# Batch 0's queries and keys as whole float32 in the score products

## The chip, the core and the metric

The kernel runs on one core of a Trainium2 chip. The core has TensorE (matrix products, PE in the rows, its weight loads PEld), VectorE (DVE), ScalarE (ACT), GpSimd (POOL), SyncE (SP, which issues most DMAs) and 16 DMA engines. The metric is the device time of one execution in microseconds. It was run three times; the median counts.

## The reference

Attention with a sparse softmax over 4 batches, 8 heads, 576 positions and 64 dimensions, then two MLP layers on the 2304 tokens. What matters here is the first lines:

```python
scale = 1.0 / np.sqrt(q.shape[-1])
scores = scale * np.matmul(q, k.transpose(0, 1, 3, 2))
thresh = np.max(scores, axis=-1, keepdims=True) - tau
scores = np.where(scores >= thresh, scores, -1000000000.0)
scores = scores - np.max(scores, axis=-1, keepdims=True)
attn = np.exp(scores)
attn = attn / (np.sum(attn, axis=-1, keepdims=True) + 1e-09)
return np.matmul(attn, v).astype(np.float32)
```

Since scores are cut at a threshold of 0.02 below a row's maximum, they have to be nearly as exact as float32. Behind this stand `h = x @ w_in; g = h * clip(h + 3, 0, 6) / 6; g @ w_out` and a second layer with `g = h - tanh(h)`.

## The kernel before

**Units.** Attention goes by units of 128 queries of one head against all 576 keys. The 512 main queries of a head are four units; the last 64 queries of two heads j of a pair make one leftover unit (`h is None`). A batch has 36 units, in two halves g = 0 and 1 of the main queries: for each g and each pair of heads j, four units, and with g = 1 a leftover unit. There are 144 units.

**Queries and keys.** TensorE turns q and k so that the 64 dimensions lie on partitions (`k_round`, `q_round`, `q_left_round`; lines 561 and 577, PSUM tile tp). From tp they are split into two parts of type float32r, a high one (ScalarE, lines 584 and 591) and the rest (VectorE, lines 586 and 593). For k, both parts of a head lie on 128 partitions, 64 each. For q, GpSimd first copies the 64 columns beside themselves (line 554), so that after turning all 128 partitions hold the same queries twice; tile q holds the high part and the rest one behind the other. A product of 128 partitions with 288 columns then adds high q times high k and high q times the rest of k; a second one does the same with the rest of q. So a unit has four pieces on TensorE: two parts of q times two halves of 288 keys (line 678). A leftover unit has eight. Leftover queries go to tile qs, whose unused columns are zero.

**Softmax of a unit.** `softmax` writes the scores to one of two PSUM buffers s. VectorE reduces them to a negative maximum z (line 683), ScalarE makes the exponentials e with z as bias (line 685) and, for the first 54 units, the threshold (line 688); VectorE keeps the exponentials at or above the threshold (line 694), which is the last reader of s. ScalarE and GpSimd split e into two float16 parts pp (lines 699 and 705), a DMA turns them (pt<-pp, line 708), and `weighted` multiplies with v (line 731).

**What else runs.** `load_w` reads the 16 weight pieces of the first layer's first half; VectorE takes four operations of 512 columns for each (lines 418 to 426), while batch 0 is in work. From `layer1` on (lines 489 and 850), TensorE does the first half of the first layer for each half batch, between the units of later batches. The second half of the first layer and the second layer follow from about 490 us on.

**Order.** Every step is recorded as a task with an engine, a duration and a due time (`add`); `Plan.issue` runs a list scheduling with those numbers and emits the instructions in the order that comes out. The hardware runs each engine's instructions in that order; buffers in rings (`Ring`) make a task wait for the users of the buffer before.

Of the kernel before, what the change touches and what calls it, by code (L numbers as in the profile page):

```python
# [9 lines left out]
F32 = mybir.dt.float32  # L10
# [20 lines left out]
class Buf:  # L31


    def __init__(self, ring, prev):
        self.ring, self.prev, self.users, self.writers = ring, prev, [], []
        self.tile, self.slot, self.ends = None, None, []

    @property
    def t(self):
        if self.tile is None:  # L40
            self.tile = self.ring.make() if self.slot is None else self.ring.make(self.slot)
        return self.tile


# [156 lines left out]
def attention_moe_moe_kernel(  # L201
# [54 lines left out]
    add = plan.add  # L256

    LAG = 4
    STEP, SLOW, KNEE = 3.0, 0.8, 4
    LK, LQ, LV, LD = 5, 3, 1, 4  # L260
    XL, FO = 1, 7
# [259 lines left out]
    def load_q_left(b, half, key):  # L521

        t = QL[b, half] = R_ql.new()
        hs = slice(half * NP, (half + 1) * NP)
        for r in range(2):
            add("dma", 0.65, key, lambda r=r: nc.sync.dma_start(
                out=t.t[:, :, r, :], in_=q[b, hs, SM:S, :].rearrange("h p d -> p h d")), w=[t], xfer=0.37, slack=SB)

    def load_k(b, j, key):
        t = KR[b, j] = R_kr.new()  # L530
        add("dma", 0.6, key, lambda: nc.sync.dma_start(
            out=t.t, in_=k[b, 2 * j:2 * j + 2, 0:SM, :].rearrange("h (p c) d -> p h c d", c=NC)), w=[t], xfer=0.88, slack=SB)

# [11 lines left out]
    def load_q(b, g, j, key, eng="dma"):  # L545

        t = QR[b, g, j] = R_qr.new()
        queue = nc.sync if eng == "dma" else nc.scalar
        for i in range(2):
            add(eng, 0.47, key, lambda i=i: queue.dma_start(  # L550
                out=t.t[:, i, :, 0, :],
                in_=q[b, 2 * j + i, 0:SM, :].rearrange("(p c) d -> p c d", c=NC)[:, 2 * g:2 * g + 2, :]), w=[t], xfer=0.37, slack=SB)
        copy = lambda r: t.t[:, :, :, r, :].rearrange("p h c d -> p (h c) d")
        add("pool", 0.5, key + 4, lambda: nc.gpsimd.tensor_copy(copy(1), copy(0)), r=[t], w=[t])

    def transposes(ps, srcs):

# [6 lines left out]
    def k_round(b, j, part, key):  # L564

        if part == 0:
            KS[b, j] = R_k.new()
        ks, tp, kr, kl = KS[b, j], R_tp.new(), KR[b, j], KL[b]
        half = (slice(0, 64), slice(64, 128))
        n = (SM // 2, LF)[part]  # L570

        def tr():
            if part == 0:
                transposes(tp.t, [(kr.t[:, i, c:c + 2, :], 0) for i in range(2) for c in (0, 2)])
            else:
                for i in range(2):
                    nc.tensor.transpose(tp.t[0:64, i * LF:(i + 1) * LF], kl.t[:, 2 * j + i, :], ident[0:LF, 0:LF])

        add("pe", 2 * n * 0.00085, key, tr, r=[kr] if part == 0 else [kl], w=[tp, ks])
        for x in range(2 - part):  # L580
            cols = slice(x * n, (x + 1) * n) if part == 0 else slice(SM, S)
            out = lambda up, cols=cols: ks.t[half[up], :, cols]
            src = lambda x=x: tp.t[half[x], 0:2 * n].rearrange("p (i n) -> p i n", i=2)
            hi = add("act", t_act(2 * n), key + RK, lambda x=x, out=out, src=src: nc.scalar.activation(
                out=out(x), in_=src(), func=ACTF.Copy), r=[tp], w=[ks])
            add("dve", t_dve(2 * n), key + RK, lambda x=x, out=out, src=src: nc.vector.tensor_tensor(
                out=out(1 - x), in0=src(), in1=out(x).bitcast(F32), op=ALU.subtract), r=[tp], w=[ks], after=[hi])
# [8 lines left out]

    def q_round(b, g, j, key):

        qr, tp, qt = QR[b, g, j], R_tp.new(), R_q.new()
        add("pe", 4 * 0.11, key, lambda: transposes(  # L600
            tp.t, [(qr.t[:, i, c, :, :], 0) for i in range(2) for c in range(2)]), r=[qr], w=[tp, qt])
        q_split(qt, tp, lambda x: qt.t[:, x], 256, key)
        QT[b, g, j] = qt

    def q_left_round(b, j, key):

        ql, tp, qt = QL[b, 2 * j // NP], R_tp.new(), R_qs[j % 2].new()
        add("pe", 2 * 0.06, key, lambda: transposes(
            tp.t, [(ql.t[:, (2 * j + i) % NP, :, :], LF) for i in range(2)]), r=[ql], w=[tp, qt])
        q_split(qt, tp, lambda x: qt.t[:, x].rearrange("p (i n) -> p i n", n=LF)[:, 0:3:2, :], LF, key)  # L610
        QT[b, "l", j] = qt
# [50 lines left out]
    def softmax(u, key):  # L662
# [8 lines left out]
        s = lambda: ps.t[:, :, 0:SH]  # L671
        ex = lambda: e.t[:, n, :].rearrange("p (a s) -> p a s", a=2)

        def scores():
            ops = [(queries(b, g, j, x, c, part), KS[b, j].t[:, x % 2]) for x in hs for part in range(2)]
            for i, (l, ks) in enumerate(ops):
# [2 lines left out]
                        ps.t[:, half, 0:SH], l, ks[:, half * SH:(half + 1) * SH], start=i == 0, stop=i == len(ops) - 1,  # L679
                    )  # L680

        add("pe", 0.53 * len(hs), key, scores, r=[KS[b, j], QT[b, g if h is not None else "l", j]], w=[ps])
        add("dve", 0.69, key, lambda: nc.vector.tensor_reduce(  # L683
            out=z.t[:, 0:1], in_=s(), axis=AX.XY, op=ALU.max, negate=True), r=[ps], w=[z])
        exp = add("act", 0.66, key, lambda: nc.scalar.activation(  # L685
# [911 lines left out]
```

## Time and profile before

| | us |
|---|---|
| median of 3 runs | 1088.65 |
| runs | 1088.2 to 1093.36 |
| the profiled execution | 1088.51 |
| its span, first to last instruction | 1086.7 |
| TensorE busy in it | 1015.0 (93%) |
| VectorE busy | 847.6 (78%) |
| ScalarE busy | 718.6 (66%) |
| GpSimd busy | 339.0 (31%) |

Busy times are from the profiled execution and don't count waiting. The granted clock (PEclk) is the share of full speed that TensorE's clock had; its two levels are 1.2 and 2.4 GHz, so a mean between 0.5 and 1 is a mix. The mean of the whole execution is 0.964. In the 40 equal slices of the span, TensorE's granted clock stands at 0.6 to 0.8 in some of the first, and at 0.9 or more from the sixth on.

### The profile page before, as it was taken

What the parts mean: (1) busy time and instruction counts of PE and PEld (TensorE: products, weight loads), DVE (VectorE), ACT (ScalarE), POOL (GpSimd) and SP (SyncE); (2) the same over time, 40 slices, a digit from 0 to 9 for tenths busy, and PEclk for the clock granted to TensorE, in tenths of its full rate; (3) what the DMA queues carried; (4) which work ended last, traced back from release to release, by engine and by line L of the source; (5) the groups of instructions that cost most, each with busy time, mean ns of one, the idle gap of its engine ahead of it and who ended that gap; (6) DMA issues with size and microseconds to landing.
All of it is one profiled execution on the core that took longest, in us unless ns stands there. A gap on an engine that the chain in (4) does not pass through costs nothing.

```text
span 1086.7 us, 23294 instructions
## 1 busy us (share of the span) xinstructions
PE 1015.0 (93%) x8984; PEld 838.6 (77%) x8984; DVE 847.6 (78%) x1630; ACT 718.6 (66%) x1312; POOL 339.0 (31%) x353
## 2 busy tenths in 40 slices
PE   5668799999999899988999999999999999999998
PEld 4557788998999799978988888876676666666664
DVE  5889977687869788758797778889976796784564
ACT  6867979687967786645675566756755675574332
POOL 2656757666855675623000000000001111121000
PEclk8668899999999989998999999999999999999999
DMA  7899688967899989978657755432333866573335
GB/s 184 165 222 213 132 159 182 196 132 158 187 181 192 205 175 216 219 159 261 201 173 257 253 199 185 165 108 97 107 117 118 208 131 117 126 127 51 87 92 142
DMA packets 285007, 179.27 MB, mean 165 GB/s; under 512 B 202976, under 2 KB 257760, under 8 KB 284896
## 3 DMA queue, kind: packets, MB, share of 16 engines
q1 hardware_dynamic: 279088, 168.07, 61.0%
q0 software_dynamic: 5184, 9.44, 6.5%
q8 instruction: 71, 1.16, 0.5%
q14 instruction: 40, 0.33, 0.1%
q10 hardware_dynamic: 624, 0.26, 0.1%
HBM read 89.13 MB, written 46.14 MB: 124 GB/s over the span
## 4 chain that ended last, share of the span: by engine, by line
PE 58%; DVE 4%; ACT 1%; DMA 1%; issue 0%; SPq 0%; ACTq 0%; DVEq 0%
PE ya L489 24%; PE m L489 16%; PE h L489 10%; PE m L850 3%; PE s L678 2%; PE tp L731 1%; DMA y<-y 1%; PE h L850 1%; PE m L476 0%; DVE x L1276 0%; DMA st<-in_moe_w_in_dram 0%; DVE xh L1048 0%; DVE t L803 0%; PE tp L561 0%; DVE y L1175 0%
## 5 line engine op out<-in xcount | busy, mean ns | idle before, releaser
L705 POOL TENSOR_TENSOR pp<-e,pp 128x128 f16<-128x128 f32 (+3 forms) x156 | 181.1, 1182 | 120.3 <-issue 54.1
L489 PE MATMUL ya<-wo,g 128*128 128x512 f16 x864 | 205.4, 379 | 1.0 <-DVE g L813 0.6
L489 PEld LDWEIGHTS <-wi 128*128 128x128 f16 x1536 | 150.0, 98 | 40.4
L1416 POOL DMA_DIRECT2D po<-o x36 | 31.2, 876 | 459.7 <-ACT o L1410 459.7
L489 PEld LDWEIGHTS <-g 128*128 128x128 f16 x864 | 84.1, 98 | 79.3 <-DVE g L813 1.1
L683 DVE TENSOR_REDUCE z<-s 128x1 f32<-128x576 f32 x144 | 107.9, 753 | 45.4 <-PE s L678 44.7
L694 DVE SCALAR_TENSOR_TENSOR e<-s,z,e 128x576 f32<-128x576 f32 x144 | 115.8, 811 | 22.1 <-ACT e L685 17.1
L678 PE MATMUL s<-ks,q 128*128 128x288 f32 x512 | 105.9, 337 | 20.9 <-DVE e L694 20.1
L685 ACT ACTIVATE e<-s,z 128x576 f32<-128x576 f32 x144 | 105.0, 739 | 26.6 <-DVE z L683 20.3
L489 PE MATMUL m<-xT,ai 128*128 128x256 f32 (+1 forms) x720 | 112.8, 301 | 1.8 <-DVE st L426 0.6
L678 PEld LDWEIGHTS s<-ks,q 128*128 128x128 f32 x512 | 82.4, 212 | 29.4 <-DVE e L694 13.4
L489 PEld LDWEIGHTS m<-xT,ai 128*128 128x128 f32 x720 | 99.3, 190 | 3.7 <-DVE st L426 1.1
L489 PE MATMUL ya<-g,bo 128*128 128x256 f16 x864 | 101.1, 273 | 0.5 <-DVE g L813 0.5
L731 PE MATMUL tp<-vt,pt 128*128 128x65 f16 (+1 forms) x2240 | 88.4, 199 | 8.5 <-ACT q L591 2.4
L489 PE MATMUL m<-x,wi 128*128 128x256 f16 x768 | 95.2, 273 | 0.0
L731 PEld LDWEIGHTS <-pt 128*128 128x128 f16 (+1 forms) x2240 | 79.8, 104 | 16.7 <-DMA pt<-pp 6.0
L1381 ACT ACTIVATE t<-t,hid_s 128x512 f32<-128x512 f32 x72 | 51.6, 718 | 62.0 <-DVE t L1372 61.4
L489 PEld LDWEIGHTS <-bo 128*128 128x128 f16 x864 | 84.1, 98 | 10.6 <-issue 0.9
L489 PEld LDWEIGHTS <-bw 128*128 128x128 f16 x864 | 84.1, 98 | 10.4 <-issue 0.4
L813 DVE SCALAR_TENSOR_TENSOR g<-g,t 128x512 f16<-128x512 f16 x108 | 73.8, 686 | 20.7 <-ACT g L809 20.2
L809 ACT ACTIVATE g<-t 128x512 f16<-128x512 f32 x108 | 67.0, 624 | 33.7 <-DVE t L1383 26.0
L699 ACT ACTIVATE pp<-e 128x1152 f16<-128x1152 f32 (+1 forms) x80 | 85.1, 1064 | 5.0 <-DVE e L694 4.7
(177 smaller groups left out, 1878.0 us busy)
## 6 DMA issues: line engine op xcount, KB each, us to landing
st<-in_moe_w_in_dram SPq DMA_DIRECT2D x40, 512.0 KB, 5.0
st<-in_moe_w_out_dram SPq DMA_DIRECT2D x40, 512.0 KB, 4.4
xf<-xs SPq DMA_DIRECT2D x18, 512.0 KB, 5.2
y<-y SPq DMA_DIRECT2D x18, 512.0 KB, 3.8
po<-o POOLq DMA_DIRECT2D x36, 256.0 KB, 4.2
xs<-xT SPq DMA_DIRECT2D x8, 640.0 KB, 4.9
y<-ys SPq DMA_DIRECT2D x9, 512.0 KB, 5.9
po<-o SPq DMA_DIRECT2D x18, 256.0 KB, 2.0
```

Source lines behind the costliest of these rows:

```text
L489: nc.tensor.matmul(ps, l[a], r[b], start=first and t == 0 and i == 0, stop=last and t == 2 and i == n - 1,)
L678: nc.tensor.matmul(ps.t[:, half, 0:SH], l, ks[:, half * SH:(half + 1) * SH], start=i == 0, stop=i == len(ops) - 1,)
L683: add("dve", 0.69, key, lambda: nc.vector.tensor_reduce(out=z.t[:, 0:1], in_=s(), axis=AX.XY, op=ALU.max, negate=True), r=[ps], w=[z])
L685: exp = add("act", 0.66, key, lambda: nc.scalar.activation(out=ex(), in_=s(), func=ACTF.Exp, bias=z.t[:, 0:1]), r=[ps, z], w=[e])
L694: add("dve", 0.74, key, lambda: nc.vector.scalar_tensor_tensor(out=ex(), in0=s(), scalar=z.t[:, 1:2], in1=ex(), op0=ALU.is_ge, op1=ALU.mul ...
L699: high = add("act", t_act(w * S, sbuf=True), key, lambda: nc.scalar.activation(out=pp.t[:, 0:w, 0:S], in_=e.t[:, 0:w, :], func=ACTF.Copy), ...
L705: add(eng, dur, key, lambda src=src, dst=dst, queue=queue: queue.tensor_tensor(out=pp.t[:, 0:w, dst], in0=e.t[:, 0:w, src], in1=pp.t[:, 0: ...
L731: nc.tensor.matmul(pv.t[0:m, w_ * (D + 1):(w_ + 1) * (D + 1)], pt.t[:, n, blk, rows], vv, start=o == 0, stop=o == len(ops) - 1)
L809: hi = add("act", t_act(n, sbuf=True), key, lambda: nc.scalar.activation(out=gh(), in_=t(), func=ACTF.Copy, scale=GS2 if far else 1.0), r= ...
L813: go = lambda: nc.vector.scalar_tensor_tensor(out=gl(), in0=gh(), scalar=1.0 / GS2, in1=t(), op0=ALU.mult, op1=ALU.subtract)
L850: prev = [add("pe", t_mm(n, 1), kd, lambda p=p, l=l, r=r, m=m, s=s, ps=ps: nc.tensor.matmul(ps.t[:, 0:n], W["o", m].t[:, l, s], r[m].t[:, ...
L1381: add("act", t_act(2 * NB, sbuf=True, scalars=True), key, lambda: nc.scalar.activation(out=s_(), in_=h.t, func=ACTF.Tanh, scale=c), r=[h], ...
```

## The change

For batch 0 alone (`WHOLE = (0,)`), q and k are no longer split. Two heads of a pair are loaded beside each other (`pairs_of`, `cells`), so that one turn puts head 2j on partitions 0 to 63 and head 2j+1 on 64 to 127, and ScalarE alone takes the result out of tp into float32 tiles (names ksw and qw, in the same rings as before). A main unit is two products in float32 on the 64 partitions of its head, of 288 columns each. A leftover unit is two products on all 128 partitions; the leftover queries of the two heads stand in a block form in tile qw, whose other columns VectorE clears (`memset`). GpSimd's copy, VectorE's splits and the second load of leftover queries go. k's loads become two DMAs of one head each, in pieces of 64 values instead of 256.

```diff
     LAG = 4
+    WHOLE = (0,)
...
     def load_k(b, j, key):
         t = KR[b, j] = R_kr.new()
+        for i in range(2 if b in WHOLE else 0):
+            add("dma", 0.5, key, lambda i=i: nc.sync.dma_start(
+                out=cells(t)[:, :, i, :], in_=k[b, 2 * j + i, 0:SM, :].rearrange("(p c) d -> p c d", c=NC)), w=[t], xfer=0.44, slack=SB)
+        if b in WHOLE:
+            return
...
+    def pairs_of(t):
+        return t.t.rearrange("p i c r d -> p (i c r d)")[:, 0:4 * D].rearrange("p (c i d) -> p c i d", c=2, i=2)
+
+    def cells(t):
+        return t.t.rearrange("p i c d -> p (i c d)").rearrange("p (c i d) -> p c i d", c=NC, i=2)
+
+    def whole(ring, tag):
+        t = ring.new()
+        t.make = lambda: at_p.tile([128, 2, S] if tag == "ks" else [128, 2, 2, 256], F32, tag=tag, name=tag + "w", bufs=ring.n)
+        return t
...
     def k_round(b, j, part, key):
...
+        if b in WHOLE:
+            w = (SM, LF)[part]
+
+            def turn_whole():
+                if part:
+                    nc.tensor.transpose(tp.t[:, 0:LF], kl.t[:, 2 * j:2 * j + 2, :].rearrange("p i d -> p (i d)"), ident[0:LF, 0:LF])
+                for x, c in enumerate(() if part else ORDER):
+                    nc.tensor.transpose(tp.t[:, x * 128:(x + 1) * 128], cells(kr)[:, c].rearrange("p i d -> p (i d)"), ident)
+
+            add("pe", w * 0.00085, key, turn_whole, r=[kl if part else kr], w=[tp, ks])
+            add("act", t_act(w), key + RK, lambda: nc.scalar.activation(
+                out=ks.t[:, 0, part * SM:part * SM + w], in_=tp.t[:, 0:w], func=ACTF.Copy), r=[tp], w=[ks])
+            return
...
     def q_round(b, g, j, key):
 
+        if b in WHOLE:
+            qr, tp, qt = QR[b, g, j], R_tp.new(), whole(R_q, "q")
+            add("pe", 2 * 0.11, key, lambda: [nc.tensor.transpose(
+                tp.t[:, c * 128:(c + 1) * 128], pairs_of(qr)[:, c].rearrange("p i d -> p (i d)"), ident) for c in range(2)],
+                r=[qr], w=[tp, qt])
+            add("act", t_act(256, scalars=True), key + RK, lambda: nc.scalar.activation(
+                out=qt.t[:, 0, 0], in_=tp.t[:, 0:256], func=ACTF.Copy, scale=tau_b[:, 2:3]), r=[tp], w=[qt])
...
     def q_left_round(b, j, key):
 
+        if b in WHOLE:
+            ql, tp, qt = QL[b, 2 * j // NP], R_tp.new(), QT[b, 1, j]
+            clear = add("dve", 0.1, key, lambda: nc.vector.memset(qt.t[:, 0, 1, 0:2 * LF], 0.0), w=[qt])
...
+        def scores_whole():
+            rows = slice(0, 128) if h is None else slice(h % 2 * 64, h % 2 * 64 + 64)
+            qt, ks = QT[b, g, j].t, KS[b, j].t
+            l = qt[:, 0, 1, 0:2 * LF] if h is None else qt[rows, 0, 0, c % 2 * 128:c % 2 * 128 + 128]
+            for half in range(2):
+                nc.tensor.matmul(
+                    ps.t[:, half, 0:SH], l, ks[rows, 0, half * SH:(half + 1) * SH], start=True, stop=True)
+
...
-        add("pe", 0.53 * len(hs), key, scores, r=[KS[b, j], QT[b, g if h is not None else "l", j]], w=[ps])
+        add("pe", 0.98 if b in WHOLE else 0.53 * len(hs), key, scores_whole if b in WHOLE else scores, r=[KS[b, j], QT[b, g if h is not None else "l", j]], w=[ps])
```

The planner gets the new tasks with their durations and orders all of attention anew. Two places show it.

TensorE from the program's first product on, before the change (line 561 turns k and q, 577 the leftover keys, 628 is a sum for v, 678 the scores):

```order
L561 MATMUL tp<-ident,kr 128x128 x4
L561 MATMUL tp<-ident,qr 128x128 x4
L577 MATMUL tp<-ident,left 64x64 x4
L628 MATMUL tp<-vs,ones 128x1
L678 MATMUL s<-ks,q 128x288 x4
L561 MATMUL tp<-ident,kr 128x128 x4
L561 MATMUL tp<-ident,qr 128x128 x4
L678 MATMUL s<-ks,q 128x288 x4
L561 MATMUL tp<-ident,kr 128x128 x4
L577 MATMUL tp<-ident,left 64x64 x2
L678 MATMUL s<-ks,q 128x288 x8
```

The same place after the change (lines 606, 642 and 604 turn k, q and leftover keys, 690 is the sum for v, 741 the scores, whose two products are one main unit):

```order
L642 MATMUL tp<-ident,qr 128x128 x2
L606 MATMUL tp<-ident,kr 128x128 x4
L604 MATMUL tp<-ident,left 128x64 x2
L741 MATMUL s<-ksw,qw 128x288 x4
L690 MATMUL tp<-vs,ones 128x1
L606 MATMUL tp<-ident,kr 128x128 x4
L642 MATMUL tp<-ident,qr 128x128 x2
L604 MATMUL tp<-ident,left 128x64
L741 MATMUL s<-ksw,qw 128x288 x2
L606 MATMUL tp<-ident,kr 128x128 x4
L741 MATMUL s<-ksw,qw 128x288 x2
```

Four q turns become two, and the leftover keys of a pair one turn of 128 columns. The first scores stood behind four rows and are one unit; now they stand behind three and are two units.

VectorE from its first work on inputs on, before (586 and 593 are splits of k and q, 632 to 637 belong to v, 683 reduces and 694 masks):

```order
L586 TENSOR_TENSOR ks<-tp,ks 64x2x256 x2
L593 SCALAR_TENSOR_TENSOR q<-tp,tau_b,q 128x512
L586 TENSOR_TENSOR ks<-tp,ks 64x2x64 x2
L632 TENSOR_SCALAR vs<-tp 128x1
L634 TENSOR_SCALAR vs<-vs 128x1
L637 RECIPROCAL sv<-vs 128x2
L683 TENSOR_REDUCE z<-s 128x1 x2
L586 TENSOR_TENSOR ks<-tp,ks 64x2x256 x2
L593 SCALAR_TENSOR_TENSOR q<-tp,tau_b,q 128x512
L694 SCALAR_TENSOR_TENSOR e<-s,z,e 128x576
L586 TENSOR_TENSOR ks<-tp,ks 64x2x256
```

After (753 reduces, 764 masks, 694 to 699 belong to v):

```order
L753 TENSOR_REDUCE z<-s 128x1 x2
L694 TENSOR_SCALAR vs<-tp 128x1
L696 TENSOR_SCALAR vs<-vs 128x1
L699 RECIPROCAL sv<-vs 128x2
L764 SCALAR_TENSOR_TENSOR e<-s,z,e 128x576
L753 TENSOR_REDUCE z<-s 128x1
L764 SCALAR_TENSOR_TENSOR e<-s,z,e 128x576
L753 TENSOR_REDUCE z<-s 128x1
L764 SCALAR_TENSOR_TENSOR e<-s,z,e 128x576
```

All splits are gone, so that VectorE's first work on inputs is the reduction of the first two units.

VectorE over two units further on in batch 0, before (tiles m and st are the weight pieces, lines 418 to 426):

```order
L683 TENSOR_REDUCE z<-s 128x1 x2
L593 SCALAR_TENSOR_TENSOR q<-tp,tau_b,q 128x512
L694 SCALAR_TENSOR_TENSOR e<-s,z,e 128x576 x2
L418 TENSOR_SCALAR m<-m 128x512
L683 TENSOR_REDUCE z<-s 128x1
L420 TENSOR_SCALAR m<-m 128x512
L683 TENSOR_REDUCE z<-s 128x1
L423 SCALAR_TENSOR_TENSOR m<-st,m 128x512
L694 SCALAR_TENSOR_TENSOR e<-s,z,e 128x576
```

After, at the like place (419 to 427 are the weight pieces):

```order
L753 TENSOR_REDUCE z<-s 128x1 x2
L419 TENSOR_SCALAR m<-m 128x512
L764 SCALAR_TENSOR_TENSOR e<-s,z,e 128x576
L421 TENSOR_SCALAR m<-m 128x512
L764 SCALAR_TENSOR_TENSOR e<-s,z,e 128x576
L424 SCALAR_TENSOR_TENSOR m<-st,m 128x512
L753 TENSOR_REDUCE z<-s 128x1
L427 SCALAR_TENSOR_TENSOR st<-st,m 128x512
L753 TENSOR_REDUCE z<-s 128x1
```

The q split between two reductions and two masking steps is gone, and a step of the weights now stands between the two masking steps.

## Rows read from the trace of the kernel before

**Rows 1.** Stretches: busy us (instructions) of PE, PEld, DVE, ACT, POOL; clock, DMA share, GB/s.

```profile
10.00:80.00 70.00, 47.80 (x344) 40.02 (x342) 59.59 (x101) 54.87 (x105) 39.02 (x35) 0.66 0.89 194
80.00:120.00 40.00, 32.78 (x348) 28.90 (x349) 37.91 (x64) 32.65 (x71) 28.73 (x28) 0.87 0.89 196
...
140.00:200.00 60.00, 56.45 (x630) 53.12 (x629) 46.15 (x81) 49.93 (x105) 39.77 (x39) 1.00 0.81 175
200.00:480.00 280.00, 269.01 (x3042) 255.89 (x3037) 215.66 (x431) 207.23 (x388) 170.88 (x174) 0.99 0.88 182
```

**Rows 2.** Waits, 10 to 80 us: who waited for whom, us, times, longest.

```profile
PE s L678 <- DVE e L694: 10.9, 10, 2.6
...
DVE z L683 <- PE s L678: 5.0, 10, 1.9
```

**Rows 3.** Timeline: start us, us, instruction, [idle before and its releaser].

```profile
64.28 2.71 PE L678 MATMUL s<-ks,q 128*128 128x288 f32 x8 [1.12 <-DVE e L694]
...
67.03 0.76 DVE L683 TENSOR_REDUCE z<-s 128x1 f32<-128x576 f32 x1 [0.22 <-PE s L678]
...
69.16 1.54 DVE L694 SCALAR_TENSOR_TENSOR e<-s,z,e 128x576 f32<-128x576 f32 x2 [0.71 <-ACT z L688]
...
70.12 2.26 PE L678 MATMUL s<-ks,q 128*128 128x288 f32 x8 [1.56 <-DVE e L694]
...
75.84 2.26 PE L678 MATMUL s<-ks,qs 128*128 128x288 f32 x8 [2.61 <-DVE e L694]
```

**Rows 4.** Groups by line, 0 to 112 us; a line's durations; a timeline row.

```profile
L561 PE MATMUL tp<-ident,qr 128*128 128x128 f32 x32 | 7.6, 383 | 0.4 <-issue 0.3
...
L586 DVE TENSOR_TENSOR ks<-tp,ks 64x512 fp32r<-64x512 f32 x10 | 6.9, 689 | 4.0 <-ACT ks L584 3.8
L593 DVE SCALAR_TENSOR_TENSOR q<-tp,tau_b,q 128x512 fp32r<-128x512 f32 x8 | 6.0, 744 | 0.1
...
L586 DVE TENSOR_TENSOR ks<-tp,ks 64x128 fp32r<-64x128 f32 x4 | 1.1, 284 | 0.6 <-ACT ks L584 0.5
...
L593 DVE SCALAR_TENSOR_TENSOR qs<-tp,tau_b,qs x3: 340/342/343, 35.6 to 89.2; 128x128 fp32r<-128x128 f32 x3
...
4.24 0.30 DVE L880 MEMSET qs<- 128x128 f32 x2
```

**Rows 5.** Timeline of TensorE: a unit's scores and what follows, at either clock level.

```profile
47.78 1.30 PE L678 MATMUL s<-ks,q 128*128 128x288 f32 x4
48.88 1.76 PE L731 MATMUL tp<-vt,pt 128*128 128x65 f16 x28
...
119.04 0.69 PE L678 MATMUL s<-ks,q 128*128 128x288 f32 x4
119.57 0.28 PE L628 MATMUL tp<-vs,ones 128*128 128x1 f32 x2
```

**Rows 6.** Line 628, all of the span: records, ns min/median/max, first and last start.

```profile
L628 PE MATMUL tp<-vs,ones x32: 164/250/372, 10.1 to 391.5; 128*128 128x1 f32 x32
```

**Rows 7.** Timeline of the start.

```profile
8.91 0.75 DVE L593 SCALAR_TENSOR_TENSOR q<-tp,tau_b,q 128x512 fp32r<-128x512 f32 x1
...
10.51 1.31 PE L678 MATMUL s<-ks,q 128*128 128x288 f32 x4
...
11.86 0.76 DVE L683 TENSOR_REDUCE z<-s 128x1 f32<-128x576 f32 x1 [0.52 <-PE s L678]
...
14.53 0.76 DVE L683 TENSOR_REDUCE z<-s 128x1 f32<-128x576 f32 x1 [1.91 <-PE s L678]
```

**Rows 8.** DMA issues, 10 to 80 us: count, KB each, median us to landing.

```profile
kr<-in_k_dram SPq DMA_DIRECT2D x3, 256.0 KB, 4.2
```

**Rows 9.** Timeline of TensorE: scores on 128 partitions, then transposes from 64.

```profile
215.81 1.22 PE L678 MATMUL s<-ks,qs 128*128 128x288 f32 x8
216.95 0.33 PE L561 MATMUL tp<-ident,left 64*128 64x64 f32 x2
```

More of the change, by code (lines that the diff above doesn't have):

```diff
@@ L35, in __init__ @@
         self.ring, self.prev, self.users, self.writers = ring, prev, [], []
-        self.tile, self.slot, self.ends = None, None, []
+        self.tile, self.slot, self.ends, self.make = None, None, [], None
     @property
@@ L40, in t @@
         if self.tile is None:
-            self.tile = self.ring.make() if self.slot is None else self.ring.make(self.slot)
+            self.tile = self.make() if self.make else self.ring.make() if self.slot is None else self.ring.make(self.slot)
         return self.tile
@@ L524, in load_q_left @@
         hs = slice(half * NP, (half + 1) * NP)
+        if b in WHOLE:
+            add("dma", 0.65, key, lambda: nc.sync.dma_start(
+                out=t.t.rearrange("p h r d -> p (h r) d")[:, 0:NP, :], in_=q[b, hs, SM:S, :].rearrange("h p d -> p h d")),
+                w=[t], xfer=0.37, slack=SB)
+            return
         for r in range(2):
@@ L548, in load_q @@
         queue = nc.sync if eng == "dma" else nc.scalar
+        if b in WHOLE:
+            for i in range(2):
+                add(eng, 0.47, key, lambda i=i: queue.dma_start(
+                    out=pairs_of(t)[:, :, i, :],
+                    in_=q[b, 2 * j + i, 0:SM, :].rearrange("(p c) d -> p c d", c=NC)[:, 2 * g:2 * g + 2, :]), w=[t], xfer=0.37, slack=SB)
+            return
         for i in range(2):
@@ L566, in k_round @@
         if part == 0:
-            KS[b, j] = R_k.new()
+            KS[b, j] = whole(R_k, "ks") if b in WHOLE else R_k.new()
         ks, tp, kr, kl = KS[b, j], R_tp.new(), KR[b, j], KL[b]
@@ L570, in k_round @@
         n = (SM // 2, LF)[part]
+        if b in WHOLE:
[8 more added lines that the diff above has]
+                out=ks.t[:, 0, part * SM:part * SM + w], in_=tp.t[:, 0:w], func=ACTF.Copy), r=[tp], w=[ks])
+            return
         def tr():
@@ L597, in q_round @@
     def q_round(b, g, j, key):
+        if b in WHOLE:
+            qr, tp, qt = QR[b, g, j], R_tp.new(), whole(R_q, "q")
[4 more added lines that the diff above has]
+                out=qt.t[:, 0, 0], in_=tp.t[:, 0:256], func=ACTF.Copy, scale=tau_b[:, 2:3]), r=[tp], w=[qt])
+            QT[b, g, j] = qt
+            return
         qr, tp, qt = QR[b, g, j], R_tp.new(), R_q.new()
@@ L605, in q_left_round @@
     def q_left_round(b, j, key):
+        if b in WHOLE:
+            ql, tp, qt = QL[b, 2 * j // NP], R_tp.new(), QT[b, 1, j]
+            clear = add("dve", 0.1, key, lambda: nc.vector.memset(qt.t[:, 0, 1, 0:2 * LF], 0.0), w=[qt])
+            add("pe", 0.06, key, lambda: nc.tensor.transpose(
+                tp.t[:, 0:LF], ql.t.rearrange("p h r d -> p (h r d)")[:, 2 * j % NP * D:(2 * j % NP + 2) * D], ident[LF:2 * LF, LF:2 * LF]),
+                r=[ql], w=[tp, qt])
+            for i in range(2):
+                half = slice(i * 64, i * 64 + 64)
+                add("act", t_act(LF, scalars=True), key + RK, lambda i=i, half=half: nc.scalar.activation(
+                    out=qt.t[half, 0, 1, i * LF:(i + 1) * LF], in_=tp.t[half, 0:LF], func=ACTF.Copy, scale=tau_b[half, 2:3]), r=[tp], w=[qt], after=[clear])
+            QT[b, "l", j] = qt
+            return
         ql, tp, qt = QL[b, 2 * j // NP], R_tp.new(), R_qs[j % 2].new()
```

## The prediction

> **What bounds the kernel now.** I read the stretches of the profile first, since one busy share over 1087 us mixes stages with different limits. From 200 to 480 us TensorE works 269 of 280 us at clock 0.99, and from 140 to 200 us 56.45 of 60 at 1.00: there the end is set by how much TensorE still has to do. From 10 to 80 us, nearly all of batch 0's attention, it works only 47.80 of 70 us, and at a granted clock of 0.66, a mix of the 1.2 and the 2.4 GHz level. VectorE has 59.59 of 70 us there and 37.91 of 40 from 80 to 120 us [rows 1]. So the change, which lies wholly in batch 0, takes work from the engine that is full and gives work to the one that has room.
>
> Next the waits. From 10 to 80 us the scores waited 10.9 us in ten places for VectorE's masking step (e, line 694), which frees their PSUM buffer; VectorE's reductions waited 5.0 us for scores [rows 2]. The two form a loop, and the timeline shows a lap: eight score pieces (two units) start at 64.28, VectorE reduces the second unit at 67.03, ScalarE's exponential and threshold come between, masking starts at 69.16 and the next eight pieces at 70.12; the lap after starts at 75.84. That is 5.84 and 5.72 us for two units, 2.9 us a unit [rows 3]. A lap holds VectorE's work and the scores' own time. Shortening the first and lengthening the second is exactly what the change does, so the two have to be weighed against each other.
>
> **What is removed from VectorE.** In batch 0 go eight k splits of 512 columns at 0.689 us, four of 128 columns at 0.284, eight q splits at 0.744 and four for leftover queries at 0.342 [rows 4]: 5.5 + 1.1 + 6.0 + 1.4 = 14.0 us. Added are four clears of 128 columns; two like them took 0.30 us [rows 4], so 0.6 us. Net 13.4 us. By VectorE's order two of the large and two of the small k splits and one q split stand ahead of the first reduction: 2 x 0.689 + 0.744 + 2 x 0.284 = 2.7 us. Six large and two small k splits, five q and two leftover splits follow before the 20th masking step, which the trace has at about 77 us: with two clears, 4.1 + 0.6 + 3.7 + 0.7 - 0.3 = 8.8 us. Two q splits, two leftover splits and two clears remain after it: 1.9 us.
>
> **What TensorE gets.** A unit of 128 queries has four pieces of 288 columns today and needs two products in whole float32. Today's pace: four pieces at 47.78 are followed by the next work at 48.88, 1.10 us at 1.2 GHz; at 119.04 and 119.57, 0.53 us at 2.4 GHz [rows 5]. No row shows a wide float32 product. The narrow one of line 628 is 16 instructions in the program and 32 records in the trace [rows 6], so one product is two records and a unit stays at four. From below, a record costs no more than today's piece: then nothing is added. From above it costs twice that. I take the upper end: today each piece fills 128 partitions with the halves of one operand, so two stationary loads cover the four partial products of 64 rows each; the new product has 64 partitions of plain values, and the same four partial products need twice the streamed columns. A unit is then 1.06 us at the high level and 2.20 at the low. The four leftover units are unchanged: eight pieces for two heads become two products over all 128 partitions, 8 x 0.13 = 1.06 either way. So 32 x 0.53 = 17.0 us is added if all runs at 2.4 GHz and 32 x 1.10 = 35.2 us if at 1.2. Sixteen q transposes of 128 columns go, 0.24 us each as this stretch ran them [rows 4], 3.8 us; the leftover ones go from 24 to 12 and are left out.
>
> The Trainium skill (FP8 and Floating Point Precision, section TensorE Precision Notes) says true FP32 is four passes through the array. By it two products of 288 columns would be 2304 columns, 0.96 us at 2.4 GHz, an estimate; that would make the addition 13.8 instead of 17.0 us.
>
> **Which clock.** With 20 units' scores added, TensorE's 47.80 us of 70 become about 62 to 66. The trace shows a stretch with 32.78 of 40 us busy at clock 0.87 and those above 90% at 0.99 to 1.00 [rows 1], so I expect 10 to 80 us at about 0.87. A score unit is then 1.06 / 0.87 = 1.2 us. Today at 0.66 it lies between 0.53 and 1.10, about 0.9. It grows by 0.3 us, not by 1.1.
>
> **The sum.** *Start:* the first scores stand at 10.51, behind a q split that ends at 9.66 and k splits, and the reductions at 11.86 and, after a wait of 1.91, at 14.53 [rows 7]. With the splits gone the scores come some 2 us earlier; they then take about 1 us longer for the first unit, and k comes by two DMAs whose second issue costs some half microsecond. Of 2.7 us I enter 1.0. *10 to 80 us:* 8.8 us less on VectorE. With two score buffers, 0.3 us more per unit lengthens the lap of two units by 0.3, so 0.15 a unit and 3.0 us for 20. Net 5.8. *80 to 120 us:* 1.9 us less on VectorE, but here the first MLP layer already shares TensorE: 32.78 us plus 16 x 0.53 = 8.5, less about 4 from the clock going from 0.87 to 1.0, is 37 of 38 us. It fills up; I enter 0. Together 6.8 us. Behind that TensorE is full and its instructions for batches 1 to 3 and the layers are the same, so the shift is carried to the end: 1088.5 us of the profiled execution (span 1086.7 and 1.8 around it) become 1081.7. The median of the runs is 1088.65, 0.1 us from it.
>
> **Entered at nothing.** ScalarE loses half of its eight wide k copies and half the columns of the q copies and gets four small ones; it has 54.87 of 70 us [rows 1] and gains at most what VectorE doesn't need. GpSimd loses eight q copies of its 39.02 of 70. The k loads come in 256-byte pieces instead of 1 KB: 256 KB took 4.2 us to land [rows 8], issued well ahead of their use; only the first pair is waited for. Below nothing is excluded, since the bytes are the same; if the DMA engines, at 0.89 from 10 to 80 us [rows 1], are filled by the extra pieces, up to 2 us are lost. The planner orders all of attention anew, since it holds other durations; rows like those of the kernel before can move by a wait or two of 1 to 3 us in either direction, which the range holds.
>
> A switch of the array also has to be priced. Between eight score pieces at 215.81 and transposes of 64 partitions at 216.95 [rows 9], 8 x 0.132 = 1.06 us of streaming ends at 216.87: the switch costs at most 0.08 us, and 64 switches 5 us of TensorE time, inside the room above. The Trainium skill (TensorEngine Tiling (Array Packing), section Key Properties) has a rule against this change: changing the tiling mode drains TensorE. By the row that drain would take 5 us out of the forecast's room and at worst out of the gain; the trace neither shows a longer one nor scores on 64 partitions.
>
> **Rivals.**
> *The whole relief comes through* (0.15). Float32 records are no longer than today's pieces, so laps shrink by all of VectorE's work: 1.0 + 8.8 + 1.9 = 11.7 us, 1076.8 us. For it: two records, as the trace has. Against it: the four partial products above.
> *The scores take it all back* (0.25). The change does what it says, but the clock stays at 0.66: a unit's scores go from 0.9 to about 1.8 us, 0.45 per unit in the lap, 9 us over 20 units against 8.8. With the start's 1.0 left, about 1088 us. For it: TensorE still waits in every lap, which is when the low level was granted. Against it: it waits less than before.
> *TensorE becomes the bound* (0.17), the slower one. At 1.2 GHz, 10 to 80 us needs 47.80 + 20 x 1.10 - 3 = 66.8 us, and the 10.9 us of waiting for the masking step [rows 2] can't be filled in program order: 77.7 instead of 70, 7.7 us later. In 80 to 120 us another 5 of the 6.5 us added don't fit, since its idle time lies in waits too. Less 1.0 at the start, 1088.5 + 11.7 = 1100 us. It decides once TensorE is over 95% busy in 10 to 80 us with the clock below about 0.7.
> *The forecast* (0.43): 1081.7 us, its own range 1078 to 1086.
>
> **The numbers.** A difference under 0.5%, 5.4 us, can't be told from none by this measurement: 1083.2 and 1094.1 are the limits. Of the forecast's 0.43 some 0.32 lie below 1083.2; with 0.15 of the first rival and a trace of the second that makes 0.48 faster. The rest of the forecast and most of the second give 0.33 for no change. The third and a little of the second give 0.19 slower. The range runs from 1075 to 1097: it cuts a little of the first rival and about half of the third.
>
> **What would show it.** VectorE about 13 us less in all, nearly all before 120 us. Two records per float32 score product, a unit's four at about 1.06 us at the high level. Granted clock of 10 to 80 us above 0.8. The first reduction before 11.5 us, and 20 masking steps done near 71 us instead of 77. TensorE's total changed by less than the 17 us, since the rest of batch 0 runs at the higher clock. The forecast is wrong if TensorE isn't full from about 130 us on, if laps stay at 2.9 us a unit, or if a wait of several microseconds appears behind batch 0 that isn't there now.

## The result, and the profile after

The changed kernel takes 1103.3 us (median of 6 runs, 1102.4 to 1105.21), the kernel before on the same chip 1089.33 (1088.2 to 1093.36): 1.0126 times as long, 95% interval 1.0107 to 1.0144, or 14 us more. The forecast was 1081.7, its range 1075 to 1097. The third rival, "TensorE becomes the bound", had said 1100.

The stretches of the profile after, columns as in [rows 1]:

```profile
10.00:80.00 70.00, 58.74 (x275) 36.85 (x275) 45.08 (x78) 46.98 (x92) 32.93 (x26) 1.00 0.77 166
80.00:120.00 40.00, 35.98 (x266) 26.27 (x265) 32.49 (x53) 26.72 (x59) 23.02 (x22) 1.00 0.74 166
...
140.00:200.00 60.00, 56.76 (x637) 53.37 (x637) 44.32 (x80) 52.16 (x110) 43.23 (x42) 0.98 0.75 161
```

From 10 to 80 us VectorE fell from 59.59 to 45.08 us busy and TensorE rose from 47.80 to 58.74; neither is full, and fewer VectorE instructions fit into the stretch (78 instead of 101). The waits of the same 70 us, against [rows 2]:

```profile
DVE z L753 <- PE s L741: 25.6, 15, 5.6
...
PE s L741 <- DVE e L764: 9.1, 8, 2.3
```

VectorE's reductions now wait 25.6 us for scores, where they waited 5.0; the scores wait about as long for the masking as before. A lap of one unit shows why (timeline of TensorE and VectorE, against [rows 3]):

```profile
15.06 2.28 PE L741 MATMUL s<-ksw,qw 64*128 64x288 f32 x4
17.27 1.11 PE L606 MATMUL tp<-ident,kr 128*128 128x128 f32 x4
...
18.92 2.29 PE L741 MATMUL s<-ksw,qw 64*128 64x288 f32 x4 [0.53 <-DVE e L764]
...
21.24 0.76 DVE L753 TENSOR_REDUCE z<-s 128x1 f32<-128x576 f32 x1 [2.38 <-PE s L741]
21.91 0.81 DVE L764 SCALAR_TENSOR_TENSOR e<-s,z,e 128x576 f32<-128x576 f32 x1
...
22.78 2.29 PE L741 MATMUL s<-ksw,qw 64*128 64x288 f32 x4 [0.53 <-DVE e L764]
```

Scores start at 18.92, are reduced at 21.24, the unit before them is masked at 21.91 (it stands behind the reduction in VectorE's order), and the next scores start at 22.78: 3.86 us a unit, 2.2 of them scores. Before it was 2.9.

One number in these rows misleads. The clock reads 1.00 from 10 to 120 us, but the durations are those of 1.2 GHz: four transposes take 1.11 us at 17.27, and a score unit 2.2 us. In the kernel before, four transposes take 1.09 us where its clock reads 0.50:

```profile
22.81 1.09 PE L561 MATMUL tp<-ident,qr 128*128 128x128 f32 x4 [0.32 <-issue]
```

Here is TensorE later in the profile of the changed kernel:

```profile
116.10 1.20 PE L741 MATMUL s<-ksw,qw 64*128 64x288 f32 x4
117.23 1.02 PE L801 MATMUL tp<-vt,pt 128*128 128x65 f16 x28
...
119.60 0.60 PE L589 MATMUL tp<-ident,kr 128*128 128x128 f32 x4
```

The same four records take 1.13 us to the next start, and four transposes 0.60. By durations the high level was first granted near 110 us, and before the first record of a change the view shows 1.00. In the kernel before this touches only the time up to some 15 us: its 0.66 from 10 to 80 us would be about 0.62 (an estimate, with those 5 us counted as 0.50).

The start, against [rows 7], and the records of line 741, against [rows 6]:

```profile
9.99 0.76 DVE L753 TENSOR_REDUCE z<-s 128x1 f32<-128x576 f32 x1 [5.60 <-PE s L741]
...
11.91 0.76 DVE L753 TENSOR_REDUCE z<-s 128x1 f32<-128x576 f32 x1 [1.16 <-PE s L741]
```

```profile
L741 PE MATMUL s<-ksw,qw x144: 402/684/847, 7.7 to 144.8; 64*128 64x288 f32 x128, 128*128 128x288 f32 x16
```

The first two reductions come 1.9 and 2.6 us earlier; 72 products are 144 records, as said. Landmarks, with the masking steps counted in VectorE's rows:

| | first reduction | 20th masking ends | 36th (batch 0's last) | 144th | span |
|---|---|---|---|---|---|
| before | 11.86 | 77.6 | 137.1 | 475.0 | 1086.7 |
| after | 9.99 | 86.3 | 149.3 | 488.5 | 1100.6 |

Batch 0 lost 14 us from its start to its end; behind it the loss stayed between 11 and 15.

### The profile page after: what moved, and what is told of

Same layout as the page of the kernel before. It is cut to its first block, busy times and chain, and to the rows that moved or that the text cites. A ratio compares the mean times of both kernels' runs of the same rounds, so it can differ in the third digit from the quotient of the medians.

```text
span 1100.6 us, 23154 instructions
## 1 busy us (share of the span) xinstructions
PE 1047.0 (95%) x8944; PEld 845.1 (77%) x8944; DVE 837.7 (76%) x1610; ACT 714.3 (65%) x1312; POOL 333.9 (30%) x345
## 4 chain that ended last, share of the span: by engine, by line
PE 53%; DVE 2%; ACT 1%; issue 0%; ACTq 0%; DVEq 0%
PE ya L490 25%; PE m L490 14%; PE h L490 10%; PE m L920 2%; PE h L920 1%; PE m L477 1%; PE tp L801 1%; PE s L748 0%; DVE t L1442 0%; DVE x L1346 0%; ACT x L1344 0%; PE m L470 0%; DVE t L1453 0%; ACT t L1451 0%; DVE g L883 0%
## 5 line engine op out<-in xcount | busy, mean ns | idle before, releaser
L490 PE MATMUL m<-xT,ai 128*128 128x256 f32 (+1 forms) x720 | 115.3, 306 | 1.3 <-DVE t L873 0.8
L490 PEld LDWEIGHTS m<-xT,ai 128*128 128x128 f32 x720 | 101.6, 195 | 4.5 <-DVE t L873 2.3
L801 PE MATMUL tp<-vt,pt 128*128 128x65 f16 (+1 forms) x2240 | 90.7, 202 | 3.9 <-DVE q L634 2.2
L741 PE MATMUL s<-ksw,qw 64*128 64x288 f32 (+1 forms) x144 | 68.8, 628 | 14.5 <-DVE e L764 13.4
L748 PE MATMUL s<-ks,q 128*128 128x288 f32 x384 | 72.3, 313 | 8.1 <-DVE e L764 7.6
```

What stands on the lines that cost most here:

```text
L490: nc.tensor.matmul(ps, l[a], r[b], start=first and t == 0 and i == 0, stop=last and t == 2 and i == n - 1,)
L741: nc.tensor.matmul(ps.t[:, half, 0:SH], l, ks[rows, 0, half * SH:(half + 1) * SH], start=True, stop=True)
L748: nc.tensor.matmul(ps.t[:, half, 0:SH], l, ks[:, half * SH:(half + 1) * SH], start=i == 0, stop=i == len(ops) - 1,)
L801: nc.tensor.matmul(pv.t[0:m, w_ * (D + 1):(w_ + 1) * (D + 1)], pt.t[:, n, blk, rows], vv, start=o == 0, stop=o == len(ops) - 1)
```

## Experiments: what kept the clock low

The theory after this profile: products on 64 of the array's 128 partitions left TensorE at the low level. First the changed kernel with one line other, every engine's order kept; each unit gets the sum of two heads' scores:

```diff
-            rows = slice(0, 128) if h is None else slice(h % 2 * 64, h % 2 * 64 + 64)
+            rows = slice(0, 128)
```

> The changed kernel in the same order on every engine; only its float32 score products of batch 0 take all 128 partitions instead of 64, so that each unit gets the sum of the scores of two heads (this part of the output is not the reference's). Theory, half-filled array: products on 64 partitions leave TensorE at the low level, and at 128 partitions it gets the high one as in the kernel before; a score unit falls from 2.2 to about 1.1 us in most of 20 to 110 us and the time to about 1080 to 1086 us, as I had forecast. Rival, doubled columns and the order: rows don't matter, the unit stays at 2.2 us until 110 us and the time within 2 us of 1103.

Measured: 1088.23 us (10 runs, 1084.41 to 1092.11), 0.997 of before (0.9949 to 0.999). Its stretches:

```profile
10.00:80.00 70.00, 48.63 (x354) 33.52 (x353) 57.09 (x96) 54.65 (x111) 41.52 (x33) 0.85 0.90 197
80.00:120.00 40.00, 34.51 (x324) 28.41 (x322) 37.86 (x64) 34.06 (x75) 27.17 (x29) 0.92 0.90 210
```

The clock rises from 11 us on, and the 36th masking ends at 131.8 instead of 149.3. That is the whole loss and 5.3 us more, from partitions alone. TensorE is even less busy from 10 to 80 us than in the changed kernel (48.63 against 58.74 us), so its idle time is not what had kept the clock low. The time is 2 us above the range I gave: not all of the 5.3 arrive at the end.

Then the products by themselves, with no other engine between them (`s` alternates between two pairs of PSUM banks; `half` are the two halves of the partitions):

```python
for u in range(U):        # stretch 1: halves in turn; 2: all 128; 3: half[0] alone
    for x in range(2):
        nc.tensor.matmul(s[u % 2][:, x, 0:SH], weights[0][half[u % 2], :], kw[half[u % 2], ends[x]], start=True, stop=True)
```

> A kernel of its own that computes nothing of the reference: five stretches of score-like products on TensorE alone, back to back, each after some 20 us of rest: 24 units of two float32 products of 288 columns on 64 partitions (halves of the array in turn), the same on 128 partitions, on 64 partitions of one half; then 48 units of two float32r products on 64 partitions in turn and on 128. Theory, half-filled array: the first, third and fourth stay at 1.2 GHz to their end (2.2 us a float32 unit, 0.55 a float32r one), the second and fifth start so and go to half of it (1.1 and 0.28) within a few microseconds. Rival, only the gaps between the products kept the clock low: all five speed up when nothing interrupts them.

Busy us (records) of TensorE and its clock in each stretch, cut where the clock changes:

```profile
16.80:21.30 4.50, 4.50 (x19) 1.00 0.00 0
21.30:31.00 9.70, 9.70 (x80) 1.00 0.01 2
44.80:48.60 3.80, 3.77 (x8) 0.50 0.01 2
48.60:70.20 21.60, 21.60 (x89) 1.00 0.00 0
83.30:129.80 46.50, 46.44 (x96) 0.50 0.00 0
```

The third stretch shows it most plainly: 46.44 us without a gap on one half of the array, and the clock stays at 0.50 to the end, 0.48 us a record, 1.93 a unit. On 128 partitions it rises early, and a record then takes 0.243 us, a unit 0.97. The first stretch missed my expectation: two halves in turn run at the same time, 19 records in 4.5 us at the low level and 80 in 9.70 at the high, 0.12 each, and the clock rises. (The 1.00 of its first 4.5 us is again the view before a first record.) The fourth, float32r in turn, missed it in the same way; the second and the fifth came as expected. The Trainium skill (TensorEngine Tiling (Array Packing), section Key Properties) says that tiles operate independently; the first stretch agrees (0.12 us a record in turn, 0.243 on 128 partitions).

Does more work around them help? The changed kernel with two products on all partitions behind each unit:

```diff
+            for half in range(2):
+                nc.tensor.matmul(ps.t[:, half, SH:512], qt[:, 0, 0, 0:128], ks[:, 0, 0:512 - SH], start=True, stop=True)
```

> The changed kernel in its own order; behind each whole score unit of batch 0 stand two float32 products of 224 columns on 128 partitions, whose result nobody reads. That is 0.78 of a unit's columns on top, 1.7 us a unit at 1.2 GHz and 0.85 at 2.4. Theory, the clock follows how much of the array works: with these the high level is granted from early on, a unit with its filler takes about 1.9 us, less than the 2.2 of the changed kernel without it, and the time is 1092 to 1103. Rival, products on 64 partitions run at that pace whatever stands around them: a unit takes 3.9 us, and with 36 units the time is above 1140.

Measured: 1127.48 us (2 runs), between the two expectations. At 64.17 a unit takes 2.22 us to the filler and the filler 1.65; the high level first comes near 57 us instead of 110, and does not stay. Inconclusive: the rise came earlier, but not early enough to pay.

## Experiments: what a score unit's length is worth

The changed kernel in its own order with q and k rounded to float32r, each product twice (four pieces a unit) and once (two); both leave out the low halves:

```diff
-[128, 2, S] if tag == "ks" else [128, 2, 2, 256], F32, tag=tag
+[128, 2, S] if tag == "ks" else [128, 2, 2, 256], F32R, tag=tag
-            for half in range(2):
+            for n, half in ((0, 0), (0, 1), (1, 0), (1, 1)):     # once: ((1, 0), (1, 1))
```

> The changed kernel in the same order, but q and k of batch 0 are rounded to one float32r value each and every score product is made twice on 64 partitions, so that a unit has four pieces of 288 columns as before the change (the low halves of q and k are left out). Theory, doubled time of scores: a unit takes 0.53 to 1.1 us, VectorE keeps its relief, and the time is 1077 to 1084. Rival, the loads in 256-byte pieces and the new order: these stay, and the time stays above 1095. If 64 partitions keep the clock low, units show 1.1 us up to 100 us, not 0.53.

> The changed kernel in its own order with q and k of batch 0 rounded to one float32r value, each product made once: a unit has two pieces of 288 columns on 64 partitions (the low halves are left out). Theory, a lap of two units holds one unit's scores: at the low level a unit takes 0.55 us, where four pieces take 1.1 and the whole float32 ones 2.2; half of 0.55 us x 36 units, 10 us, moves the 36th masking step from 131.2 to about 122 us. Rival, VectorE is full again once the scores are short: it stays at 127 to 131 us.

Twice: 1089.18 us, 0.9987 of before (0.9966 to 1.0009). Once: 1080.8 (5 runs), 0.9917 (0.988 to 0.9953). Both stay at the low level to about 80 or 90 us; a unit then takes 1.25 and 0.78 us to the next work, more than expected. The 36th masking ends at 131.2 and 126.1. The time of the first and the masking of the second lie between theory and rival. This clears the loads in 256-byte pieces and the order, which are the changed kernel's in both: with shorter scores batch 0 is 6 to 11 us quicker than before. What TensorE works on the scores of batch 0 (line 741) in the changed kernel, in the first and in the second, then its clock (which reads 1.00 too long here as well), DMA share and GB/s:

```profile
0.00:150.00 150.00, 68.84 (x144) 0.99 0.77 170
0.00:150.00 150.00, 41.05 (x144) 0.99 0.86 187
0.00:150.00 150.00, 26.50 (x72) 0.95 0.88 192
```

The first step takes 27.8 us from the scores and moves batch 0's end by 18.1, 0.65 us for each microsecond; the second takes 14.6 and moves it by 5.1, 0.35. VectorE, as busy as before the change, is probably the next limit; no run tests it:

```profile
10.00:80.00 70.00, 44.54 (x342) 32.87 (x340) 59.99 (x100) 58.05 (x119) 45.24 (x37) 1.00 0.96 207
```

The other way round, the kernel before with each score product of batch 0 twice on its 128 partitions:

```diff
-... for x in hs for part in range(2)]
+... for x in hs for part in range(2)] * (2 if b == 0 else 1)
```

> The kernel before in its own order, each score product of batch 0 made twice (the sums come out doubled), so that a unit has eight pieces of 288 columns on 128 partitions: TensorE gets the columns that the change added, VectorE keeps its splits. Theory, clock: filled partitions and more work raise the clock, a unit takes about 1.1 us, and the time rises by 2 to 8 us, 1091 to 1097. Rival, doubled columns cost the same whatever the rows: the clock stays near 0.66, a unit takes about 2 us, laps grow by 0.5 us a unit, and the time rises by 15 us or more, above 1104.

1104.33 us, 1.012 (1.0096 to 1.0144); clock 0.80 from 10 to 80 us, 36th masking at 150.0. The rival's time, though not its clock: with VectorE still at its splits, 21.7 us more of scores (64.7 instead of 43.1 us of TensorE) cost 13 us at batch 0's end, 0.60 for each, even at 0.80 instead of 0.66. Scores of nearly equal length stand in the kernel before (43.1 us, 36th masking at 137.1) and in the one with four float32r pieces (41.1 us, 131.2): there the missing splits and the new order are worth some 5 us (an estimate: 5.9, less 0.65 for each of the 2 us). The relief is real; longer scores take it.

## Experiments: the order of the instructions

> The changed kernel, but the planner is told 2.2 us for a whole score unit instead of 0.98, and orders all anew. Theory, wrong duration in the plan: VectorE has reductions of the next unit ahead of the masking of the last, waits 27.7 us for scores in 10 to 120 us, and a lap is scores 2.3 + reduction 0.76 + masking 0.81 = 3.9 us a unit; with the masking ahead it is nearer to 3 us a unit, the waits fall to below 15 us, and the time to 1088 to 1095. Rival, the length of the scores alone: two score buffers and 2.2 us hold the lap in any order, 1100 to 1105.

The edit is one number, 0.98 to 2.2 in the scores' task. 1097.23 us, 1.0065 (1.0039 to 1.0092): the time lies between theory and rival. VectorE's wait for scores from 10 to 80 us falls from 25.6 to 14.0 us, the 36th masking ends at 143.6, and the unit still takes 2.2 us:

```profile
DVE z L753 <- PE s L741: 14.0, 8, 5.7
```

The wrong duration in the plan is thus about 6 of the 14 us; with it right, the rest stays.

The two heads as a pair of units, products in turn on the two halves, and the same with one head's products after the other's:

```diff
+            for half in range(2):
+                for p, rows in ((ps, slice(0, 64)), (ps2, slice(64, 128))):
+                    nc.tensor.matmul(p.t[:, half, 0:SH], qt[rows, ...], ks[rows, ...], start=True, stop=True)
```

> The changed kernel with the units of batch 0 in pairs: the same 128 queries of the two heads of a pair, whose products are issued in turn on the two halves of the array, into the two score buffers. The stretches of products alone showed such pairs at 0.95 us a unit at 1.2 GHz and 0.49 at 2.4, and the clock rising, against 1.93 for one half and no rise. Theory, half-filled array: TensorE is then as quick as before the change and VectorE keeps its relief of 13 us; batch 0's 36th masking step ends at 126 to 132 us (before 137, changed 149) and the time is 1078 to 1086. Rival, the shorter scores are worth nothing because both buffers must come free together: laps stay at 3 us a unit or more, 1090 to 1100.

> The same paired kernel, with the two heads' products one after the other instead of in turn: the two of the first head, then the two of the second. Every other instruction stands where it stood. Theory: the halves then work mostly one at a time, a pair takes 3.5 to 4.4 us at the low level, the clock stays low through most of batch 0, and the time is 1096 to 1112. Rival, the pairing of the units and the new order do it, not the two halves at once: within 3 us of the paired kernel.

1098.41 and 1098.01 us, 1.0065 (1.0043 to 1.0088) and 1.0062 (1.0041 to 1.0083). The rival of each held. A pair takes 2.9 to 3.6 us at the low level in either order: less than two units behind each other (3.9), but far from the 1.9 of the products alone, so in the kernel the halves overlap only in part; why is open. And though both halves work, the clock stays at the low level from 41 to 82 us. What the pair loses stands in a lap of it:

```profile
43.14 2.98 PE L748 MATMUL s<-ksw,qw 64*128 64x288 f32 x8 [0.26 <-DVE e L773]
...
45.44 1.49 DVE L762 TENSOR_REDUCE z<-s 128x1 f32<-128x576 f32 x2 [1.72 <-PE s L748]
...
47.15 1.36 ACT L764 ACTIVATE e<-s,z 128x576 f32<-128x576 f32 x2
...
49.22 1.54 DVE L773 SCALAR_TENSOR_TENSOR e<-s,z,e 128x576 f32<-128x576 f32 x2 [2.16 <-ACT z L767]
...
50.09 3.01 PE L748 MATMUL s<-ksw,qw 64*128 64x288 f32 x8 [1.09 <-DVE e L773]
```

Nothing overlaps: scores, both reductions, both exponentials and both maskings follow each other, 6.95 us for two units.

Next, complete scores on 128 partitions: each head's q in columns of its own, zeros on the other 64 partitions (a GpSimd clear and a second ScalarE copy for each q round). First planned anew, then in the changed kernel's order, then with VectorE making the threshold:

```diff
+            clear = add("pool", 0.6, key, lambda: nc.gpsimd.memset(flat_q(qt.t)[:, 0:512], 0.0), w=[qt])
-                out=qt.t[:, 0, 0], in_=tp.t[:, 0:256], ...
+                out=flat_q(qt.t)[half, i * 256:i * 256 + 256], in_=tp.t[half, 0:256], ...     # for both halves
```

> The changed kernel with every float32 score product on 128 partitions: each head's q stands in columns of its own whose other 64 partitions GpSimd fills with zeros, so k of both heads can be streamed and the scores are the reference's. It costs ScalarE a second q copy and GpSimd a clear of 512 columns for each of eight q rounds. Theory, half-filled array: the clock rises early as in the run with 128 partitions that added two heads up, batch 0's 36th masking step ends near 132 us instead of 149 (before: 137), and the time is 1084 to 1089, 14 to 19 us under the changed kernel. Rival: it was the length or the order of the scores, and the time stays above 1098.

> As the kernel with each head's q in columns of its own and zeros on the other 64 partitions, but the planner is not told of the clears and the second copies: every engine keeps the changed kernel's order, with eight clears on GpSimd (0.52 us) and eight copies on ScalarE (0.47 us) put in. Theory, clock and order: the scores are those of the run that added two heads up, so the 36th masking step ends at 132 to 136 us (there 131.8, with the other order 146.0), and the time is 1086 to 1092. Rival, the clear and the copies themselves cost what that order seemed to cost: 142 us or later and above 1097.

> The kernel with zeros on the other 64 partitions in the changed kernel's own order once more, for a profile of an ordinary execution; its time was 1097.7 (1091 to 1104). Theory, order: the 36th masking step ends at 132 to 138 us and what is lost is lost behind batch 0. Rival, the clears and copies: it ends at 140 us or later.

> As the kernel of the run before, but the threshold of batch 0 (z, 0.28 us on ScalarE behind the exponential) is made by VectorE (0.15 us) ahead of it, planned anew. Theory, a loop of waits: what counts in batch 0 is the time from scores to masking, not how full VectorE is; 0.28 us less in each unit moves the 36th masking step 4 to 8 us ahead and the time to 1080 to 1087. Rival: the new order's waits decide and eat it, 1088 to 1100.

1102.73 us, 1.0111 (1.0071 to 1.0151); 1097.7, 1.0064 (1.0028 to 1.01), and 1102.74 in the single run that its profile shows; 1098.33, 1.0069 (1.0047 to 1.0091). The clock from 10 to 80 us is 0.84, 0.68 and 0.85, and the 36th masking ends at 146.0, 143.6 and 137.2. I had said 132, 132 to 138, and 4 to 8 us ahead of the second; only the third of these came, and it gave nothing in the time. Nor is it firm, since the second's profile is of an execution 5 us above that kernel's median. In the changed kernel's order (second version) the clears sit in the loop (waits from 10 to 140 us):

```profile
DVE z L762 <- PE s L750: 22.2, 18, 6.2
PE s L750 <- DVE e L773: 21.1, 16, 3.1
...
ACT qw L652 <- POOL qw L649: 8.1, 3, 4.9
```

ScalarE's q copy waits 8.1 us for three clears queued behind GpSimd's other work, and TensorE in turn waits 3.7 us for such copies. That these waits cost the clock (0.68 where the run with 128 partitions has 0.85) is an argument, no run shows it. The first and the third have that run's clock, and scores about as long (55.7 and 52.5 us of TensorE, there 52.7), and still end batch 0 some 14 and 5 us later than its 131.8: the loss lies in what their new orders wait for, and which wait it is stays open.

## Experiments: where TensorE is full

> The change in batch 1 instead of batch 0, where TensorE is full and at the high level and VectorE is not the bound. Theory: every microsecond that the scores grow is lost; 32 units x 0.53 less 3.8 of q transposes, 13 us, if the clock holds: 1098 to 1106; if the clock falls to the low level while these products run, 1110 to 1125. Rival, VectorE's relief counts there too: within 4 us of the kernel before.

> The paired kernel with all four batches in whole float32. Theory: a pair of units then costs TensorE as much as before the change and each further batch loses 16 transposes of about 0.12 us, 2 us a batch where TensorE is full; 0 to 6 us below the kernel that pairs batch 0 alone. Rival, as the change in batch 1 alone did (24 us): whole float32 where TensorE is full costs 10 us or more a batch.

> The kernel with q and k rounded to one float32r value and each score product made once (the low halves are left out), in all four batches instead of the first. Theory, TensorE full: behind batch 0 each unit gives back what TensorE saves, 32 units x 0.26 and 4 leftover units x 0.53 and 2 us of transposes, 12 us a batch, 36 us in three: 1042 to 1052. Rival, the loop of waits from scores to masking takes over there as in batch 0: 1058 to 1078.

The change in batch 1 alone: 1114.42 us, 1.0231 (1.0195 to 1.0267), 24 us instead of 13; this is in the range given for a clock that falls, but the rows there show the high level (TensorE's timeline of it):

```profile
201.36 1.24 PE L741 MATMUL s<-ksw,qw 64*128 64x288 f32 x4
202.53 1.02 PE L801 MATMUL tp<-vt,pt 128*128 128x65 f16 x28
```

The unit of 1.17 us is 0.64 more than 0.53, 20 us over 32 units, some 17 less the transposes that go; the 72nd masking is 16 us late. The 144th is 21 late, and where the rest arises is open. Paired in all batches: 1103.05, 1.0116 (1.009 to 1.0142), 5 us above batch 0 alone; neither expectation is met. Rounded and once in all batches (low halves left out): 1075.59, 0.9854 (0.9822 to 0.9886), the rival's range. Behind batch 0 the 108 units take 330.8 us instead of 338.0: 7 of the 36 us expected. From 200 to 480 us TensorE is busy 259.30 of 280 us, and the transposed exponentials (pt) arrive late in eleven places, 8.8 us. So a unit's growth costs there in full, a saving is not given back in full; why so little of it is, stays open.

## Why the prediction was wrong, step by step

- *VectorE's relief, 13.4 us.* Right: the splits that went, less the clears, are 13.3 us. VectorE's total fell by 9.9 only (837.7 against 847.6), since other instructions took longer.
- *Two records per product, 1.06 us a unit at the high level and 2.20 at the low.* Right: 1.13 and 2.2 us in the kernel, 0.97 and 1.93 back to back. The switch of the array, put at 0.08 us or less, is near it: behind a unit's last record the next instruction starts after 0.33 us at the high level and 0.62 at the low one, where two records of a unit start 0.24 and 0.48 apart, so 0.09 and 0.14 us. TensorE's total was to grow by less than 17 us; it grew by 32 (1015.0 to 1047.0).
- *The start, 1.0 us.* The first reduction came 1.9 us earlier.
- *Which clock.* The step that failed. I expected 0.87 from 10 to 80 us, since TensorE would be busier and [rows 1] show a higher clock with a busier TensorE; a unit would be 1.2 us. TensorE got busier (58.74 of 70), and yet the high level did not come until 110 us: 25 of the 36 units took 2.2 us. But the score products behind those rows fill all partitions. The change halves them, and the run with 128 partitions in the same order and the stretch of 46.44 us at 0.50 show that this, not idle time, made the difference. The Trainium skill (TensorE: Matmul & The Clock Gate, Part 1) ties the clock to how busy the PE has been; the trace of the products alone differs, since an engine without a gap for 46.44 us stayed at 0.50.
- *The lap's half, 0.15 us for 0.3.* The right size on the whole: 0.65, 0.60 and 0.35 in the runs above. With 52.7 us of scores (128 partitions) or 41.1 (float32r), the order of the changed kernel moves batch 0's end 5.3 or 5.9 us ahead; my sum had 6.8 with units of 1.2, 43 us. With the 68.8 us that they took it ends another 18 us later (149.3 against 131.8 or 131.2), and the sum changes its sign. (The 16 us of scores saved on 128 partitions are worth more than 0.65 each; there TensorE's other work ran faster too.) In its terms: I entered 3.0 us for longer scores. TensorE worked 25.8 us more on those of batch 0 (68.8 against 43.1), at 0.65 some 17 us. That is 14 of the 19 us between the 6.8 ahead that I forecast and the 12.2 behind at the 36th masking; the plan's 6 make up the rest (an estimate).
- *The planner, "a wait or two of 1 to 3 us".* Too small: one number in the plan is worth 6 us, the second part of the miss.
- *TensorE full behind batch 0, so the shift is carried to the end.* Right for a delay (12.2 us at the 36th masking, 13.5 at the 144th, 14 in the time). A lead is partly lost: 5.3 us became about 1.5 with 128 partitions (4.5 of it are still there at the 144th masking), 5.9 under 1 with float32r products made twice, while 10.9 became 9 where they are made once. The traces have stretches at the low level of 3 to 14 us at the ends of batches, longer here and there, at other places in each kernel (in the kernel before two slices behind the sixth stand at 0.8 for this, not at 0.9 as I wrote); that these eat the lead is an argument, no run shows it.
- *The rivals.* The third named price and place: the low level in 10 to 80 us and 1100 us. Its condition, TensorE over 95% busy, was not met (84%); a loop of waits at the low level is enough. The second had the low clock too, but priced a unit at a mix of the levels. I gave the third 0.17, since I took the clock to follow busy time.

## What to carry to other kernels

Before work is moved to TensorE, look at how many of its partitions each instruction fills: a record of 288 columns took 0.48 us at 1.2 GHz on 64 as on 128, and the products on 64 left the engine at that level for 100 us here. Check a clock row against a known duration, and price a stretch whose waits form a loop by the lap's terms at both levels. No version here with complete scores beats the kernel before; those clearly below it leave out the low halves of q and k.

## What was not expected of the hardware

Products on opposite halves of the array overlap when nothing stands between them: 0.12 us a record of 288 columns in turn, 0.243 on 128 partitions, at the high level. In the kernel the overlap was partial. One half alone never left the low level in 46.44 us without a gap. And the clock's rows read 1.00 until the first change is recorded: over 100 us in the changed kernel, at durations of 1.2 GHz.
